# A decode kernel's down projection as row-streaming matmuls, with the last residual formed in four rows

## The chip, the cores and the metric

The kernel runs on one core of one Trainium2 chip. The metric is device time in microseconds of one execution. The engines are TensorE (PE; its weight loads are PEld), VectorE (DVE), ScalarE (ACT), GpSimd (POOL) and SyncE (SP). SyncE issues all the large loads. PSUM is the memory that TensorE writes its results to; a partition is one of the 128 rows of the on-chip memories. The granted clock is the share of TensorE's full clock that the profile shows. In the profile's lines, SPq and ACTq are the queues of SyncE and ScalarE, here with a DMA that they issue, and "issue" is time in which an engine waited for nothing that the profile shows. kt_sb is a large buffer that holds several small tiles of the changed kernel.

## The reference, cut to what matters

One token passes through adaptive layer norm, attention over a cache of 65,536 keys with 4 key/value heads, and a gated feed-forward block. Only the end of it matters here:

```python
x = x + ga * A_ref(h, ...)                       # attention, all before the change
h = layernorm(x) * (1 + cb) + sb
x = x + gb * ((gelu(h @ w_gate) * (h @ w_up)) @ w_down)     # w_down: 3584 x 1024, bf16
```

The result is one vector of 1024 bf16 numbers, 2 KB.

## The kernel before

The gate and up projections already work by rows: the activation column sits in a weight block of 32 columns (one used, 31 zero), the weight matrix's row is streamed against it 512 columns at a time, and four such matmuls go to the four groups of 32 PSUM partitions (four column tiles). The down projection does not: each 128x128 block of `w_down` is loaded as the stationary operand and meets a single column.

```python
def col_matvec(bank, jobs, rhs, ready, nblk):            # the down projection before
    ...
    for (jb, view, k0, nk) in jobs:
        PE.wait(jb.tok)                                  # this load has landed
        for kk in range(nk):
            for j in range(nblk):                        # 8 blocks of 128 columns
                ins = pe.matmul(bank[:, j:j+1], view[:, kk, j*P:(j+1)*P],
                                rhs[:, k0+kk:k0+kk+1], ...)
...
v = col_matvec(acc_dn, j_d, u_col, (v_uc,), KD)          # acc_dn: 128 x 8 in PSUM
t_dn  = acc_dn * gb_nat                                  # VectorE, 128 x 8
y_col = t_dn + x1_nat                                    # VectorE, 128 x 8
pe.transpose(b6[0:KD, 384:384+P], y_col, identf)         # to 8 rows of 128
y_row = copy(b6[0:KD, 384:384+P])                        # VectorE, to bf16
sp.dma_start(out[0, 0].rearrange("(j p) -> j p", p=P), y_row[:, :])   # partitions 0..7
```

(The last lines are simplified: the instructions are written as formulas, and the waits are left out; every step waits for the one above.) `w_down` has 28 rows of 128x1024. It comes in three loads of 8 rows (2 MB) and three small ones of 2, 1 and 1 rows. All are issued long before they land.

## Time and profile before

| | before |
|---|---|
| time, median of 3 runs | 440.44 us (440.28 to 440.68) |
| bytes read | 185.6 MB, 423 GB/s on average |
| last weight packet lands | 435.71 us |
| last down row starts on TensorE | 436.04 us |
| first VectorE instruction after it | 436.46 us |
| store issued | 437.60 us |
| end of span | 438.84 us |

Rows three to seven come from the records of DMA packets and instructions in the trace, counted from the start of the span. The store's own time, issue to end, is 438.84 - 437.60 = 1.24 us.

From the page of the kernel before: the first line gives the DMA engines' busy share in tenths of 40 slices, the last one the shares of the chain of work that ended last.

```profile
DMA  8999999999999999999999999999999999999995
...
DMA 60%; PE 35%; DVE 2%; issue 1%; SPq 1%; ACT 1%; POOL 0%
```

The DMA engines are busy at 90% or more in 38 slices of 40. Nothing that shortens TensorE's work in the middle can move the end much; only the last microseconds can.

The chain of waits of the kernel before, its end, in order of time (start us, length us, what):

```profile
404.33 29.13 DMA slots<-in_B_w_down_dram
...
433.51 2.51 PE b L372 x88
...
436.04 0.39 PE b L372 x8
...
436.46 0.18 DVE t_dn L844
...
436.66 0.18 DVE y_col L846
...
436.88 0.39 PE b L848
...
437.29 0.28 DVE y_row L850
```

The timeline of the kernel before (start us, length us, engine, line, operation, operands, shapes, count, and in brackets the idle time before and what ended it), its down groups and the store:

```profile
423.86 1.85 PE L372 MATMUL b<-u_col,slots 128*128 128x1 bf16 x64 [0.49 <-DVE u_col L841]
...
428.64 1.86 PE L372 MATMUL b<-u_col,slots 128*128 128x1 bf16 x64 [2.93 <-DMA slots<-in_B_w_down_dram]
...
433.51 2.91 PE L372 MATMUL b<-u_col,slots 128*128 128x1 bf16 x96 [3.01 <-DMA slots<-in_B_w_down_dram]
...
437.60 0.37 SPq L852 DMA_DIRECT2D out_dram<-y_row  x1
```

TensorE needs 1.85 us for 8 rows that take 4.8 us to arrive, and idles 3 us before the second and the third group. In the last group it has just caught up with the small loads. The windows view (us, busy us of each engine with its count of instructions, granted clock, DMA share, GB/s) shows the loads ending only while the last group runs:

```profile
435.50:436.00 0.50, 0.50 (x20) 0.43 (x17) 0.00 (x0) 0.00 (x0) 0.00 (x0) 0.50 0.17 49
436.00:437.00 1.00, 0.51 (x10) 0.38 (x9) 0.34 (x2) 0.00 (x0) 0.00 (x0) 0.50 0.00 0
```

So the end is a sum of steps after one event: the last weight lands; 0.34 us later the last row starts; 0.41 us later VectorE starts; 1.14 us of VectorE and transpose; 1.24 us of store.

### The profile page before, as it was taken

The page shows a single profiled execution, that of the slowest core. Times are in us where ns is not written, and L with a number is a line of the kernel's source. Part 1 is how long each engine was busy: PE and PEld are TensorE (multiplying, and loading weights), DVE is VectorE, ACT ScalarE, POOL GpSimd, SP SyncE. Part 2 cuts the span into 40 slices and gives each one's busy share as a digit, 9 for nine tenths or more (in the row PEclk, how much of TensorE's full clock was granted, in tenths as well). Part 3 has the DMA queues.
Part 4 walks back from the last instruction along what each step waited for, and adds up shares of the span by engine and source line. Part 5 has one row for each costly group of instructions (what it writes and reads, how often), then busy time and mean ns, then how long its engine had stood idle before and what let it go on. Part 6 is the DMA issues. An engine that isn't in the chain of part 4 may idle for free.

```text
span 438.8 us, 15336 instructions
## 1 busy us (share of the span) xinstructions
PE 351.7 (80%) x7107; PEld 318.4 (73%) x7107; DVE 176.2 (40%) x300; ACT 146.4 (33%) x553; POOL 11.7 (3%) x25
## 2 busy tenths in 40 slices
PE   0547449998989889898799989999989999557554
PEld 0214139998989879798799989899988999434234
DVE  4102013545444644455444466345563365142100
ACT  1000001343435634344613553444654434600000
POOL 8100000000000000000000000000000000000000
PEclk9955555959777986869955899556995597659855
DMA  8999999999999999999999999999999999999995
GB/s 332 427 435 428 430 429 432 432 433 425 430 445 420 453 414 455 408 445 438 410 448 415 445 419 442 427 435 432 430 437 424 439 423 433 432 427 431 424 425 237
DMA packets 11957, 185.89 MB, mean 424 GB/s; under 512 B 1568, under 2 KB 1568, under 8 KB 1952
## 3 DMA queue, kind: packets, MB, share of 16 engines
q1 hardware_dynamic: 11632, 185.61, 98.8%
q8 instruction: 13, 0.21, 0.2%
q10 hardware_dynamic: 304, 0.01, 0.0%
q14 instruction: 8, 0.07, 0.0%
HBM read 185.60 MB, written 0.00 MB: 423 GB/s over the span
## 4 chain that ended last, share of the span: by engine, by line
DMA 60%; PE 35%; DVE 2%; issue 1%; SPq 1%; ACT 1%; POOL 0%
DMA slots<-in_A_v_cache_dram 39%; PE kt_ps L561 18%; DMA slots<-in_A_k_cache_dram 10%; DMA slots<-in_B_w_down_dram 7%; PE b L625 7%; PE sc_ps L581 6%; DMA slots<-in_w_mod_dram 4%; PE kt_ps L392 2%; PE b L605 1%; SPq L234 1%; PE b L372 1%; ACT p_sb L691 1%; PE b L595 1%; DVE kt_sb L751 0%; PE sc_ps L453 0%
## 5 line engine op out<-in xcount | busy, mean ns | idle before, releaser
L561 PE MATMUL kt_ps<-ident,slots 128*128 128x128 bf16 x2048 | 179.5, 258 | 11.0 <-DMA slots<-in_A_k_cache_dram 10.3
L561 PEld LDWEIGHTS kt_ps<-ident,slots 128*128 128x128 bf16 x2048 | 154.9, 118 | 12.7 <-issue 9.8
L660 DVE COPY kt_sb<-kt_ps 128x2048 bf16<-128x2048 bf16 x96 | 117.6, 1225 | 108.6 <-PE kt_ps L561 108.5
L660 ACT ACTIVATE kt_sb<-kt_ps 128x2048 bf16<-128x2048 bf16 x32 | 60.1, 1877 | 183.3 <-PE kt_ps L561 183.3
L625 PE MATMUL b<-p_sb,slots 128*128 128x8 bf16 x2176 | 75.8, 168 | 20.6 <-DMA slots<-in_A_v_cache_dram 11.2
L625 PEld LDWEIGHTS b<-p_sb,slots 128*128 128x128 bf16 x2176 | 69.8, 100 | 23.3 <-DMA slots<-in_A_v_cache_dram 12.3
L691 ACT ACTIVATE p_sb<-sc_ps,mneg 128x64 bf16<-128x64 f32 x256 | 83.5, 560 | 3.9 <-DVE mneg L686 3.9
L691 ACT ACTIVATION_READ_ACCUMULATOR p_sb<-sc_ps,mneg 128x1 f32 x256 | 77.1, 365 | 0.0
L581 PE MATMUL sc_ps<-q_buf,kt_sb 128*128 128x8 bf16 x2112 | 69.9, 167 | 0.5 <-issue 0.5
L581 PEld LDWEIGHTS sc_ps<-q_buf,kt_sb 128*128 128x128 bf16 x2112 | 67.9, 100 | 0.6 <-issue 0.6
L392 PE MATMUL kt_ps<-slots,h_pad 128*32 128x512 bf16 x176 | 17.1, 510 | 14.3 <-DMA slots<-in_A_wq_dram 6.3
L684 DVE TENSOR_REDUCE mg<-b 8x1 f32<-8x128 f32 x32 | 8.9, 279 | 37.1 <-PE b L595 37.1
L679 DVE TENSOR_REDUCE m_col<-sc_ps 128x8 f32<-128x512 f32 x32 | 21.8, 681 | 4.7 <-PE sc_ps L581 4.7
L392 PEld LDWEIGHTS kt_ps<-slots,h_pad 128*32 128x32 bf16 x176 | 5.0, 112 | 24.1 <-DMA slots<-in_A_wq_dram 8.3
L392 PE MATMUL kt_ps<-slots,s_pad 128*32 128x512 bf16 x96 | 12.5, 553 | 9.3 <-DMA slots<-in_w_mod_dram 9.3
L392 PEld LDWEIGHTS kt_ps<-slots,s_pad 128*32 128x32 bf16 x96 | 3.6, 119 | 17.3 <-DMA slots<-in_w_mod_dram 12.6
L605 PE MATMUL b<-negi,mg 8*128 8x8 f32 x66 | 15.8, 309 | 0.0
L605 PEld LDWEIGHTS b<-negi,mg 8*128 8x128 f32 x66 | 12.7, 239 | 2.2
L453 PEld LDWEIGHTS sc_ps<-identf,kt_sb 128*128 128x128 f32 (+1 forms) x48 | 7.6, 204 | 8.2 <-DVE kt_sb L774 4.3
L453 PE MATMUL sc_ps<-identf,kt_sb 128*128 128x128 f32 (+1 forms) x48 | 9.1, 352 | 4.5 <-DVE kt_sb L774 2.4
L686 DVE COPY mneg<-b 128x8 f32<-128x8 f32 x32 | 5.3, 167 | 18.1 <-PE b L605 18.1
L372 PE MATMUL b<-u_col,slots 128*128 128x1 bf16 x224 | 6.6, 165 | 6.5 <-DMA slots<-in_B_w_down_dram 5.9
(97 smaller groups left out, 84.9 us busy)
## 6 DMA issues: line engine op xcount, KB each, us to landing
slots<-in_A_k_cache_dram SPq DMA_DIRECT2D x16, 4096.0 KB, 20.3
slots<-in_A_v_cache_dram SPq DMA_DIRECT2D x32, 2048.0 KB, 26.5
slots<-in_w_mod_dram SPq DMA_DIRECT2D x8, 1536.0 KB, 17.5
slots<-in_A_wq_dram SPq DMA_DIRECT2D x4, 2048.0 KB, 35.2
slots<-in_A_wo_dram SPq DMA_DIRECT2D x4, 2048.0 KB, 32.5
slots<-in_B_w_gate_dram SPq DMA_DIRECT2D x4, 1792.0 KB, 21.9
slots<-in_B_w_up_dram SPq DMA_DIRECT2D x4, 1792.0 KB, 23.6
slots<-in_B_w_down_dram SPq DMA_DIRECT2D x3, 2048.0 KB, 29.1
```

Of the source, the lines that this page charges most:

```text
L372: ins = pe.matmul(bank[:, j:j + 1], view[:, kk, j * P:(j + 1) * P], rhs[:, k0 + kk:k0 + kk + 1], start=first, stop=True, skip_group_check= ...
L392: ins = pe.matmul(out, pad[:, k, :], jb.view[:, kk, c0:c0 + ROW], start=k <= last_k[0], stop=k >= last_k[1], skip_group_check=True,)
L453: ins = pe.transpose(dst[:, i * w:i * w + n], src[:, a], identf[0:src.shape[0], 0:n])
L561: ins = pe.transpose(kt_ps[:, half * 2048 + t * P:half * 2048 + (t + 1) * P], j_k[i - i % KU].view[:, i % KU * CH + b * TB + t, :], ident[ ...
L581: ins = pe.matmul(sc_ps[:, base + n * REP:base + (n + 1) * REP], kt_sb[:, j % 2, n, :], q_buf[:, j % SITES, :], start=True, stop=True,)
L605: ins = pe.matmul(b6[:, 256:256 + REP], mg8[:, j % 2:j % 2 + 1].to_broadcast([REP, P]), negi[:, :], start=True, stop=True,)
L625: ins = pe.matmul(b7[:, s * REP:(s + 1) * REP], j_v[j].view[:, n, :], p_sb[:, s, n, :], start=(n == 0), stop=(n == CH - 1),)
L660: ev[i % SITES][b].done(act.activation(dst, src, ACT.Copy) if E_ is AC else dve.tensor_copy(dst, src))
L679: m1[s].done(dve.tensor_reduce(m_col[:, j % 2, :].unsqueeze(2), scv, AX.X, ALU.max))
L684: m2[s].done(dve.tensor_reduce(mg8[:, j % 2:j % 2 + 1], b6[0:REP, 32:32 + P], AX.X, ALU.max))
L686: v_mc[j] = DVE.done(dve.tensor_copy(mneg[:, j, :], b6[:, 256:256 + REP]))
L691: ins = act.activation(p_sb[:, s, :, h], scv[:, h, :], ACT.Exp, bias=mneg[:, j, h:h + 1], scale=scale, accum_out=z_all[:, j, h:h + 1],)
```

## The change

The intent: the down projection works by rows too, like the other projections. Each row of `w_down` streams in four matmuls of 256 columns, one to each group of 32 PSUM partitions. The result then lies in four rows, on partitions 0, 32, 64 and 96, so it needs no transpose. The residual and its gate are turned into the same four rows ahead of time. The diff, cut to its core:

```diff
+    for n, a in enumerate((gb_nat, x1_nat)):             # ahead of time: gate and residual,
+        for h in range(2):                               # spread to columns 0, 32, 64, 96
+            v_pq = DVE.done(dve.tensor_copy(
+                pad_q[:, (2*n+h)*P:(2*n+h+1)*P:QD], a[:, h:KD:2]))
 ...
-        for dst, a, b in zip(parts(u_col), parts(g2), parts_ps()):
+        for dst, a, b in zip(parts(o_pad[:, 0:FD, 0]), parts(g2), parts_ps()):
 ...
-        v = col_matvec(acc_dn, j_d, u_col, (v_uc,), KD)
+        for n in range(4):                               # before the first down row
+            ins = pe.transpose(kt_fp[...], pad_q[:, n*P:(n+1)*P], identf[:, :])
+        v_q4 = DVE.done(dve.tensor_copy(ktf(0)[:, 4*HALF:6*HALF], kt_fp[...]))   # gb_q, x1_q
+        def place_d(k):
+            for g in range(NQ):
+                yield acc_dn[QD*g:QD*(g+1), :], g*HALF
+        v = row_matvec(place_d, j_d, o_pad, (v_uc,), (0, FD-1), width=HALF)   # HALF = 256
-        v = DVE.done(dve.tensor_tensor(t_dn[:, :], acc_dn, gb_nat[:, :], ALU.mult))
-        v = DVE.done(dve.tensor_tensor(y_col[:, :], t_dn[:, :], x1_nat[:, :], ALU.add))
-        v = PE.done(pe.transpose(b6[0:KD, 384:384+P], y_col[:, :], identf[:, :]))
-        v = DVE.done(dve.tensor_copy(y_row[:, :], b6[0:KD, 384:384+P]))
-        sp.dma_start(out[0, 0].rearrange("(j p) -> j p", p=P), y_row[:, :])
+        v = DVE.done(dve.tensor_tensor(t_q, acc_dn, gb_q, ALU.mult))      # 128 x 256
+        v = DVE.done(dve.tensor_tensor(y_q, t_q, x1_q, ALU.add))          # to bf16
+        sp.dma_start(out[0, 0].rearrange("(g n) -> g n", g=NQ), y_q[0:P:QD, :])
 ... (waits cut; several small tiles move into a large buffer that is free by then)
```

`y_q[0:P:QD, :]` reads partitions 0, 32, 64, 96.

## The prediction

> **What bounds the kernel now.** The loads. The page gives 185.9 MB at 424 GB/s mean; the DMA engines stand at 9 tenths in 38 of 40 slices, and the chain of waits is 60% DMA and 35% TensorE, the latter mostly in the attention loop, which stays. Only the last microseconds can change: the down projection and what follows.
>
> There, TensorE waits for weights. By the timeline the three large down loads are used from 423.8, 428.6 and 433.5 us. A 64-matmul group takes 1.85 us of a 4.8 us interval, so TensorE idles about 3 us before each. After 433.5 the chain of waits lists 88 matmuls (2.51 us), then the last 8 (436.04 to 436.43). These start after a small gap: the windows view shows DMA still moving 49 GB/s in 435.5–436.0 and nothing after. So even the end of TensorE's work hangs on the last weight's landing (about 435.7), not on matmul throughput. Then, serial and exposed: multiply 0.17, add 0.17, transpose 0.37, cast 0.28, with gaps 436.46 to 437.57 = 1.11 us; then the store, to 438.8.
>
> **What the change does.**
> - Removes 224 one-column matmuls (28 rows x 8, about 27 ns apart: 0.21 us a row, clock 0.5 in the windows view).
> - Adds 112 matmuls of 256 columns, four column tiles at a time. At this clock 14 of the up projection's 512-column matmuls take 1.89 us, a group of four each 0.427 us. Estimate for 256 columns: half, 0.213 us a row: a tie. The Trainium skill, "TensorE: Matmul & The Clock Gate", Part 3, says column tiles run concurrently; this trace agrees. I expect the clock to stay at 0.5: TensorE still idles 60% of each interval.
> - The last row: four 256-column matmuls, about 0.39 us (first cold 512-column matmul 0.61 less 0.21), against 0.39 for eight small ones. A tie too.
> - After it: transpose and cast go; multiply and add grow from 8 to 256 columns. The 128x256 f32 multiply at the attention's end took 0.41 us; the Trainium skill, "VectorE: DVE Perf Modes", errata section, gives (N+151)/0.96 ns, an estimate of 0.42. So 0.42+0.42+gaps = 0.88 us instead of 1.11: about -0.23 us.
> - Off the path: zeroing and four small copies (near 403.7–405, VectorE idle until 406.9), four transposes (about 0.65 us) ahead of the first down group, a 0.69 us copy. The first group ends near 426.4 instead of 425.7; the next load comes at 428.6. Free.
> - Loads, order and slot releases are unchanged, so the stream ends when it did. The store has four 512 B rows instead of eight of 256 B: no difference expected (1.2 us from issue to end).
>
> **Prediction.** 440.44 - 0.23 = 440.2 us, range 439.5 to 440.9 (before's runs spread 0.4 us). Faster by over 2%: 0.005; within 2%: 0.99; slower by over 2%: 0.005.
>
> **What would show the steps.** Down groups of 32 matmuls taking about 1.9 us, TensorE still waiting about 2.9 us for each load; two VectorE instructions of about 0.42 us after the last matmul, 0.9 us from its end to the store's issue; clock 0.5 from 413 us; last weight packet near 435.7.
>
> **What would make it wrong.** If a 256-column row took well over 0.23 us (weight loads not hidden), the last 12 rows would lag behind the landing: 0.02 us for each 2 ns of a row. At clock 1 the last row would shorten by about 0.1 us. A shift in when the 16 DMA engines finish (last packets spread over 4 us) could move the end by several tenths either way.

## The result, and the profile after

The changed kernel takes 440.79 us (median of 6 runs, 440.65 to 440.99); the kernel before 440.44 us in 6 runs (440.28 to 440.68). The ratio is 1.0009 with a 95% interval of 0.9996 to 1.0021. A ratio here is the mean time of one kernel's fast runs over that of the other's fast runs of the same rounds, so it is not quite the ratio of the medians quoted. By the 2% rule the two are the same, and the interval includes 1. But the six runs of each barely overlap (before goes up to 440.68, after starts at 440.65), and the medians moved up, not down: +0.35 us where -0.23 was forecast. The outputs are right.

The chain of waits of the changed kernel, its end:

```profile
403.28 30.59 DMA slots<-in_B_w_down_dram
...
433.91 2.95 PE b L373 x25
...
436.89 0.43 DVE kt_sb L841
...
437.35 0.42 DVE kt_sb L843
```

The transpose and the cast are gone, and the two VectorE instructions have grown as forecast. The timeline of the changed kernel, its down groups and the store:

```profile
424.46 1.42 PE L373 MATMUL b<-slots,o_pad 128*32 128x256 bf16 x32
...
429.03 1.90 PE L373 MATMUL b<-slots,o_pad 128*32 128x256 bf16 x32 [3.14 <-DMA slots<-in_B_w_down_dram]
...
433.91 2.92 PE L373 MATMUL b<-slots,o_pad 128*32 128x256 bf16 x48 [2.99 <-DMA slots<-in_B_w_down_dram]
...
437.80 0.65 SPq L845 DMA_DIRECT2D out_dram<-kt_sb  x1
```

TensorE still idles some 3 us before the second and the third group, so the four transposes in front of the first group cost nothing. The last line is the surprise: issuing the store took 0.65 us where it took 0.37. SyncE then waited for it, by its own waits view, first of the kernel before and then of the changed one:

```profile
SPq L853 <- DMA out_dram<-y_row: 0.8, 1, 0.8
```

```profile
SPq L846 <- DMA out_dram<-kt_sb: 1.0, 1, 1.0
```

The granted clock of the changed kernel (third number from the end of a line), windows view:

```profile
424.00:426.00 2.00, 1.89 (x35) 1.06 (x33) 0.78 (x3) 0.00 (x0) 0.00 (x0) 0.69 1.00 422
426.00:428.00 2.00, 0.00 (x0) 0.00 (x0) 0.00 (x0) 0.00 (x0) 0.00 (x0) 1.00 1.02 430
428.00:430.00 2.00, 0.97 (x20) 0.75 (x24) 0.00 (x0) 0.00 (x0) 0.00 (x0) 0.67 1.00 422
430.00:433.00 3.00, 0.92 (x20) 0.33 (x12) 0.00 (x0) 0.00 (x0) 0.00 (x0) 0.50 1.00 412
```

It rose for a while, by the clock's own records from 425.3 to 428.7 us: rows 5 to 8 of the first group started 0.11 us apart instead of 0.21, so that group took only 1.42 us. It was back at 0.5 before the second group began, and stayed there for the group that counts.

All kernels can be laid side by side by the steps after the last weight's landing. The times (us) are differences of records in the trace: end of the last weight packet, start of the last row's first matmul, start of the first VectorE instruction after it, issue of the store, end of the span. The table includes the experiments of the next section.

| kernel | landing | landing to row | row to VectorE | VectorE to issue | issue to end | time, median |
|---|---|---|---|---|---|---|
| before | 435.71 | 0.34 | 0.41 | 1.14 | 1.24 | 440.44 |
| before, again (e10) | 435.92 | 0.34 | 0.41 | 1.14 | 1.24 | 440.55 |
| after | 436.09 | 0.35 | 0.46 | 0.91 | 1.70 | 440.79 |
| after, again (e11) | 435.92 | 0.37 | 0.46 | 0.91 | 1.69 | 440.88 |
| e1: after, 256 B pieces | 435.98 | 0.34 | 0.46 | 0.91 | 1.75 | 440.77 |
| e2: before, rows 16 partitions apart | 435.85 | 0.39 | 0.41 | 1.26 | 1.75 | 441.29 |
| e3: before, 4 adjacent rows | 435.85 | 0.34 | 0.41 | 1.49 | 1.23 | 440.83 |
| e4: after, ScalarE's queue | 436.15 | 0.38 | 0.46 | 0.91 | 1.71 | 440.95 |
| e5: after, adjacent (wrong) | 435.81 | 0.42 | 0.46 | 0.91 | 1.24 | 440.43 |
| e6: after, 4 one-row stores | 436.17 | 0.34 | 0.46 | 0.91 | 1.69 | 440.84 |
| e7: before, residual in PSUM | 435.72 | 0.38 | 0.41 | 0.90 | 1.24 | 440.13 |
| e8: e7 and idle matmuls | 435.74 | 0.37 | 0.41 | 0.90 | 1.24 | 440.11 |
| e9: before, rows 2 partitions apart | 436.06 | 0.35 | 0.41 | 1.15 | 1.83 | 441.03 |

From before to after: last row +0.05, VectorE to issue -0.23, store +0.46, together +0.28 us. The times differ by 0.35. The remaining 0.07 is within the scatter of the landing (more on that under e10 and e11). All of the store's extra time lies before its first packet: by the records that came 0.79 us after the issue began in the kernel before and 1.25 in the changed one, and from there to the end it took 0.44 and 0.45.

### The profile page after: what moved, and what is told of

It is laid out like the page before. It is cut to its first block, busy times and chain, and to the rows that moved or that the text cites. A ratio compares the mean times of both kernels' runs of the same rounds, so it can differ in the third digit from the quotient of the medians.

```text
span 439.5 us, 15124 instructions
## 1 busy us (share of the span) xinstructions
PE 344.2 (78%) x6998; PEld 309.0 (70%) x6998; DVE 177.2 (40%) x305; ACT 146.5 (33%) x553; POOL 11.7 (3%) x25
## 4 chain that ended last, share of the span: by engine, by line
DMA 60%; PE 34%; DVE 2%; issue 2%; SPq 1%; ACT 1%; POOL 0%
DMA slots<-in_A_v_cache_dram 40%; PE kt_ps L542 17%; DMA slots<-in_A_k_cache_dram 10%; DMA slots<-in_B_w_down_dram 7%; PE b L606 7%; PE sc_ps L562 6%; DMA slots<-in_w_mod_dram 4%; PE kt_ps L373 2%; PE b L586 1%; SPq L231 1%; PE b L373 1%; ACT p_sb L672 1%; PE b L576 1%; DVE kt_sb L732 0%; PE sc_ps L434 0%
## 5 line engine op out<-in xcount | busy, mean ns | idle before, releaser
L542 PE MATMUL kt_ps<-ident,slots 128*128 128x128 bf16 x2048 | 173.3, 253 | 14.0 <-DMA slots<-in_A_k_cache_dram 13.3
L542 PEld LDWEIGHTS kt_ps<-ident,slots 128*128 128x128 bf16 x2048 | 149.2, 115 | 15.8 <-issue 10.1
L606 PE MATMUL b<-p_sb,slots 128*128 128x8 bf16 x2176 | 74.9, 167 | 23.8 <-DMA slots<-in_A_v_cache_dram 11.3
L606 PEld LDWEIGHTS b<-p_sb,slots 128*128 128x128 bf16 x2176 | 68.8, 99 | 26.6 <-issue 13.3
L586 PE MATMUL b<-negi,mg 8*128 8x8 f32 x66 | 14.9, 296 | 0.0
L757 ACT ACTIVATE kt_sb<-kt_ps 96x512 f32<-96x512 f32 (+1 forms) x3 | 1.8, 594 | 30.8 <-PE kt_ps L373 30.8
```

The source lines that it names most:

```text
L542: ins = pe.transpose(kt_ps[:, half * 2048 + t * P:half * 2048 + (t + 1) * P], j_k[i - i % KU].view[:, i % KU * CH + b * TB + t, :], ident[ ...
L586: ins = pe.matmul(b6[:, 256:256 + REP], mg8[:, j % 2:j % 2 + 1].to_broadcast([REP, P]), negi[:, :], start=True, stop=True,)
L606: ins = pe.matmul(b7[:, s * REP:(s + 1) * REP], j_v[j].view[:, n, :], p_sb[:, s, n, :], start=(n == 0), stop=(n == CH - 1),)
```

## The experiments

The theory after the first comparison: the store got dearer because its rows no longer lie on adjacent partitions. Its rivals: there are fewer rows (four instead of eight); the pieces are larger (512 B instead of 256 B); the state of SyncE's queue; chance in one profile; and, outside the store, that the wide rows on TensorE or the later landing cost the time.

A difference of 0.4 us is 0.1% of the time, and the intervals of the ratios below are some 0.13 to 0.17% on each side. So the ratios of single experiments settle next to nothing here (of all of them only e2's interval excludes 1). The steps in the trace after the last row's start repeat to about 0.02 us where nothing was changed in them.

### e1: the same four partitions, in pieces of 256 B

```diff
-    y_q = ...[:, 0:HALF]                        # 256 adjacent numbers
+    y_q = ...rearrange("p (h n) -> p h n", h=2)[:, :, 0:P]      # two runs of 128, with a gap
-        sp.dma_start(out[0, 0].rearrange("(g n) -> g n", g=NQ), y_q[0:P:QD, :])
+        sp.dma_start(out[0, 0].rearrange("(g h n) -> g h n", g=NQ, h=2), y_q[0:P:QD, :, :])
```

> The changed kernel with one edit: the store still reads partitions 0, 32, 64, 96, but each row leaves as two pieces of 256 B. The profile of the changed kernel has 1.70 us from the store's issue to the end of the span (issue 0.65), that of before 1.24 (issue 0.37). Theory 'four rows' (the cost comes with the count of four rows): still about 1.7. Theory 'spread partitions' (it comes with the step of 32 partitions): still about 1.7. Theory 'piece size' (it comes with 512 B pieces): about 1.24. Theory 'chance' (one profile was unlucky): about 1.24, and different from one run to the next.

The timeline of this kernel, the store:

```profile
437.69 0.69 SPq L848 DMA_DIRECT2D out_dram<-kt_sb  x1
```

The store stayed dear: issue 0.69 us, 1.75 us to the end; 440.77 us against 440.40 of before in the same rounds, ratio 1.0007 (0.9990 to 1.0023). The DMA records show eight packets of 256 B. Piece size alone is out, and so is chance.

### e2: the kernel before, with its rows 16 partitions apart

```diff
-    y_col = sb("y_col", [P, KD])
+    y_wide = ktf(0)[:, 0:P]                     # zeroed beforehand
+    y_col = y_wide[:, 0:P:P // KD]              # columns 0, 16, .., 112
-    y_row = sb("y_row", [KD, P], dt.bfloat16)
+    y_row = ktf(0)[:, P:2*P].bitcast(dt.bfloat16)[:, 0:P]   # in the buffer that y_q uses
-        pe.transpose(b6[0:KD, 384:384+P], y_col[:, :], identf[:, :])
+        pe.transpose(b6[:, 384:384+P], y_wide, identf[:, :])
 ... (the cast's 128 rows and the waits cut)
-        sp.dma_start(..., y_row[:, :])
+        sp.dma_start(..., y_row[0:P:P // KD, :])
```

> The kernel before with one edit: its eight rows of 256 B lie on partitions 0, 16, .., 112 instead of 0 to 7 (the transpose takes a zero-padded 128-column operand, so it may cost some 0.05 to 0.1 us more). 'Four rows': issue to end stays 1.24 us, issue 0.37. 'Spread partitions': about 1.7, issue 0.65. 'Piece size': 1.24. 'Chance': 1.24.

The timeline of this kernel, its transpose and its store:

```profile
core 0 of [0], span 439.7 us
...
437.07 0.48 PE L851 MATMUL b<-identf,kt_sb 128*128 128x128 f32 x1 [0.47 <-DVE kt_sb L849]
...
437.91 0.71 SPq L855 DMA_DIRECT2D out_dram<-kt_sb  x1
```

With the kernel before's eight rows of 256 B, its arithmetic and its down matmuls, the step between partitions took the issue from 0.37 to 0.71 us, and issue to end from 1.24 to 1.75. The rows also moved to another buffer here; e3 and e5 read adjacent partitions of that same buffer and are cheap, so the buffer is out as a cause. The wider transpose added 0.1 us, the upper end of what was expected. The time was 441.29 us against 440.40, ratio 1.0020 (1.0003 to 1.0036).

### e3: the kernel before, with four rows of 512 B on adjacent partitions

```diff
-    y_row = sb("y_row", [KD, P], dt.bfloat16)
+    y_row = ktf(0)[0:NQ, 0:P].bitcast(dt.bfloat16)          # 4 x 256, in the buffer that y_q uses
-        v = PE.done(pe.transpose(b6[0:KD, 384:384+P], y_col[:, :], identf[:, :]))
+        for h in range(2):
+            ins = pe.transpose(kt_fp[0:NQ, (8+h)*P:(9+h)*P], y_col[:, h:KD:2], identf[:, :])
+        v = PE.done(ins)
-        sp.dma_start(out[0, 0].rearrange("(j p) -> j p", p=P), y_row[:, :])
+        sp.dma_start(out[0, 0].rearrange("(j p) -> j p", j=NQ), y_row)
```

> The kernel before with one edit: the last transpose is made in two halves so that four rows of 512 B lie on adjacent partitions 0 to 3. 'Four rows': issue to end about 1.7 us, issue 0.65. 'Spread partitions': 1.24, issue 0.37. 'Piece size': about 1.7. 'Chance': 1.24. The cast of 256 columns should take about 0.42 us instead of 0.28 and the second transpose add about 0.1.

The timeline of this kernel, its cast and its store:

```profile
core 0 of [0], span 439.3 us
...
437.65 0.41 DVE L853 CAST kt_sb<-kt_ps 4x256 bf16<-4x256 f32 x1 [0.68 <-PE kt_ps L849]
438.09 0.35 SPq L855 DMA_DIRECT2D out_dram<-kt_sb  x1
```

Four rows of 512 B are as cheap as eight of 256 B when they are adjacent: 0.35 us to issue, 1.23 to the end. "Four rows" and "piece size" are out. The median was higher than before's (440.83 against 440.40; ratio 1.0009, 0.9992 to 1.0025), and the trace shows where: a second transpose and a longer cast made VectorE-to-issue 1.49 us. The cast grew as expected, but the two transposes took 0.59 us where one took 0.37, so the second cost twice the expected 0.1.

### e4: the changed kernel, store issued by ScalarE

```diff
-        SP.wait(v); sp.dma_start(...); sp.wait_ge(out_sem, 16)
+        AC.wait(v); act.dma_start(...); act.wait_ge(out_sem, 16)
```

> The changed kernel with one edit: the store is issued from ScalarE's queue, which has been idle since the up projection's eviction, instead of from SyncE's queue, which carried all the loads. If the longer store comes from the state of SyncE's queue after the loads, issue to end falls to about 1.2 us. If it comes from the shape of the store, it stays about 1.7. Also a further look at when the last weight lands in the changed kernel: 436.1 us in its one profile against 435.7 before; if that is chance, it scatters by some tenths over these four runs without regard to the kernel.

The timeline of this kernel, the store:

```profile
437.90 0.62 ACTq L845 DMA_DIRECT2D out_dram<-kt_sb  x1
```

The idle queue was no better: issue 0.62, 1.71 us to the end, 440.95 against 440.40 us. The state of SyncE's queue is out. This agrees with the Trainium skill, "DMA: Bandwidth & Descriptors", section "Issuing engines are not separate DMA queues", by which the DMAs of all issuing engines run on the same DMA engines; which of them carried this store, the trace does not show.

### e5: the changed kernel, store from adjacent partitions (wrong)

```diff
-        sp.dma_start(out[0, 0].rearrange("(g n) -> g n", g=NQ), y_q[0:P:QD, :])
+        sp.dma_start(out[0, 0].rearrange("(g n) -> g n", g=NQ), y_q[0:NQ, :])
```

Three of its four output rows hold no result. It shows what the rest of the change is worth.

> The changed kernel with one edit, wrong on purpose: the store reads partitions 0 to 3 instead of 0, 32, 64, 96, so three of the four rows hold no result; it measures what the change would be worth without the step between its partitions. 'Spread partitions': issue to end falls from 1.70 to 1.24 us (issue 0.35), the time by about 0.46 us, from 440.79 to about 440.3, a little below before (440.42). 'The wide rows on TensorE cost it' (rival: the loss sits in the matmuls or in the weights' landing, not in the store): the time stays near 440.8.

The timeline of this kernel, the last row and what follows:

```profile
core 0 of [0], span 438.8 us
...
436.23 0.41 PE L373 MATMUL b<-slots,o_pad 128*32 128x256 bf16 x4 [0.17 <-DMA slots<-in_B_w_down_dram]
436.69 0.42 DVE L841 TENSOR_TENSOR kt_sb<-b,kt_sb 128x256 f32<-128x256 f32 x1 [11.73 <-PE b L373]
437.15 0.42 DVE L843 TENSOR_TENSOR kt_sb<-kt_sb 128x256 bf16<-128x256 f32 x1
437.60 0.35 SPq L845 DMA_DIRECT2D out_dram<-kt_sb  x1
```

With the change's whole arithmetic kept, issue fell to 0.35 and issue to end to 1.24 us, about the figures of before (0.37 and 1.24). The time was 440.43 us, beside 440.48 of before in the same rounds (ratio 1.0000, 0.9987 to 1.0014) and 440.79 of the changed kernel. The rival that put the loss into the wide rows falls; what the trace leaves to them is the 0.05 us of the last row. The store's step fell by the expected 0.46 us, the median by only 0.36. In this profile the last row started 0.07 us later after the landing than in after's (0.42 against 0.35); the rest is within the spread of the five runs (440.19 to 440.66). The run also shows TensorE waiting for the last weight ("[0.17 <-DMA ...]"), so the wide rows keep up with the loads.

### e6: the changed kernel, four stores of one row

```diff
+        for E_, q, gs in ((SP, sp, (0, 1)), (AC, act, (2, 3))):
+            E_.wait(v)
+            for g in gs:
+                q.dma_start(rows[g:g+1, :], y_q[QD*g:QD*g+1, :]).then_inc(out_sem, 16)
+        sp.wait_ge(out_sem, 64)
```

> The changed kernel with one edit: four stores of one row each, two from SyncE's queue and two from ScalarE's, so that none has a step between partitions. If the step alone makes a store dear, each issue takes about 0.35 us, two in a row 0.75, and issue to end is 1.24 + about 0.38 = 1.6 us, 0.1 less than the changed kernel's 1.70. If every store from partitions 32, 64, 96 is dear whatever its step, issues take about 0.65 and issue to end is over 2.2 us.

The timeline of this kernel, its stores by queue:

```profile
437.88 0.62 SPq L848 DMA_DIRECT2D out_dram<-kt_sb  x2
437.88 0.56 ACTq L848 DMA_DIRECT2D out_dram<-kt_sb  x2
```

Each single-row issue took 0.25 to 0.32 us, even from partitions 32, 64 and 96, so those partitions are not dear in themselves; the step within one store is. But two issues in a row ate the gain: 1.69 us from issue to end, not the expected 1.6, and 440.84 us (ratio 1.0007, 0.9992 to 1.0022). By the records the end came 0.50 us after the last packet, where it took 0.36 to 0.37 in the kernels before and after. The semaphore updates in the trace show where that arose: the completions of the four stores arrived 1.11, 1.30, 1.48 and 1.66 us after the first issue, 0.18 to 0.19 us apart, although the packets of the first two had ended within 0.03 us of each other. What spaces them is open.

### e7: the kernel before, with the residual put into PSUM ahead of time

The store of before is the good one, so the search for something faster than both goes from there. The transpose is a matmul, and a matmul can accumulate: the residual is turned into rows ahead of the first down row (at 423.2 us), and the last matmul adds the scaled projection to it.

Simplified in the same way:

```diff
+        pe.matmul(b6[0:KD, 384:384+P], x1_nat[:, :], identf[:, :], start=True, stop=False, ...)
         v = col_matvec(acc_dn, j_d, u_col, (v_uc,), KD)
         t_dn = acc_dn * gb_nat                               # now rounded to bf16
-        y_col = t_dn + x1_nat
-        pe.transpose(b6[0:KD, 384:384+P], y_col[:, :], identf[:, :])
+        pe.matmul(b6[0:KD, 384:384+P], t_dn[:, :], ident[:, :], start=False, stop=True, ...)
```

> The kernel before with one edit that keeps its store: the residual is put into the transpose's PSUM rows while TensorE waits for weights (an f32 matmul against the identity), and the scaled projection, rounded to bf16, is added there by one bf16 matmul against the identity. The add (0.17 us and its gap 0.03) goes and the f32 transpose of 0.37 us becomes a cold bf16 matmul of 128 columns (estimate 0.29, from 0.39 for a cold 256-column one less 0.107). From the last matmul's end to the store's issue: about 0.85 us instead of 1.14, so about 440.1 us, 0.28 below before.

The timeline of this kernel, after the last down group:

```profile
core 0 of [0], span 438.7 us
...
436.52 0.17 DVE L845 TENSOR_TENSOR t_dn<-b,gb_nat 128x8 bf16<-128x8 f32 x1 [12.83 <-PE b L371]
...
436.74 0.27 PE L848 MATMUL b<-ident,t_dn 128*8 128x128 bf16 x1 [0.26 <-DVE t_dn L845]
437.11 0.28 DVE L851 CAST y_row<-b 8x128 bf16<-8x128 f32 x1 [0.43 <-PE b L848]
437.42 0.37 SPq L853 DMA_DIRECT2D out_dram<-y_row  x1
```

VectorE to issue fell to 0.90 us (0.85 was expected), as short as in the changed kernel, with the cheap store kept. The result is correct. The time was 440.13 us (440.01 to 440.42) beside 440.48 (440.25 to 440.57), ratio 0.9995 (0.9981 to 1.0009). The interval includes 1, so the times do not show it faster; the trace does show the step that is shorter, by 0.24 us.

### e8: e7 with idle matmuls to raise the clock

```diff
                 release(jb, tok)
+                for _ in range(fill_in[n] if n < len(fill_in) else 0):      # 6, then 7
+                    pe.matmul(kt_fp[:, 0:ROW], ident[:, :], slots[8][:, 0:ROW], ...)
```

> As the run before, and 6 and 7 idle matmuls of 512 columns into a free bank after the first two down groups, to bring TensorE's clock to 1 before the last group. If the clock rises, the last 8 matmuls take about 0.3 us instead of 0.39 and the bf16 matmul about 0.2 instead of 0.29: another 0.15 to 0.2 us, about 439.9. If the clock stays at 0.5, the idle matmuls (7 x 0.427 = 3.0 us in a wait of 3.0) can push the last group back by some tenths, and the run is slower than the one before it.

The windows view of this kernel, around the down groups:

```profile
426.00:428.00 2.00, 2.00 (x5) 0.58 (x4) 0.00 (x0) 0.00 (x0) 0.00 (x0) 0.50 1.03 434
428.00:430.00 2.00, 1.66 (x51) 1.35 (x51) 0.00 (x0) 0.00 (x0) 0.00 (x0) 0.50 0.98 406
430.00:433.00 3.00, 2.76 (x26) 1.25 (x24) 0.00 (x0) 0.00 (x0) 0.00 (x0) 0.50 0.97 401
433.00:436.50 3.50, 3.36 (x98) 2.71 (x96) 0.00 (x0) 0.00 (x0) 0.00 (x0) 0.50 0.35 136
```

The clock stayed at 0.50 although TensorE's records fill 9.78 of these 10.5 us. The steps are those of e7 and the time, 440.11 us, too (ratio 0.9995, 0.9981 to 1.0009). The idle matmuls neither helped nor pushed the last group back. What would raise the clock there is open.

### e9: the kernel before, with its rows 2 partitions apart

As e2, with a step of 2: `y_col = y_wide[:, 0:2*KD:2]`, and the store reads `y_row[0:2*KD:2, :]`.

> The kernel before with its eight rows of 256 B on partitions 0, 2, .., 14. The store of rows 16 partitions apart took 1.75 us from issue to end (issue 0.71), adjacent ones 1.24 (0.37). If any step over 1 is dear: about 1.75 again. If what is dear is that the rows lie in different groups of 32 partitions: 1.24. From the last down matmul to the store's issue about 1.15 us, as before.

The timeline of this kernel, the store:

```profile
core 0 of [0], span 439.8 us
...
437.97 0.79 SPq L855 DMA_DIRECT2D out_dram<-kt_sb  x1
```

All the rows lie within one group of 32 partitions, and still the issue took 0.79 us and issue to end 1.83. The time was 441.03 us against 440.45 (ratio 1.0011, 0.9994 to 1.0028). So it is a step of more than one partition, even 2, and not the spread over partition groups.

### e10 and e11: both kernels again, unchanged

> The kernel before, unchanged, for a second profile: store 1.24 us from issue to end, last weight at 435.7 to 435.9 if the five profiles of its family so far (435.71 to 435.85) are typical; up to 436.2 if the landing is chance alone.

> The changed kernel, unchanged, for a second profile: store 1.70 us from issue to end, 0.91 us from the last matmul to the issue, 0.46 for the last row. The five profiles of its family so far have the last weight at 435.81 to 436.17; near 436.1 would mean that these builds' loads run some 0.2 us late from the start, near 435.8 that it is chance.

Every step after the last row's start repeated to within 0.01 us (table above). The last weight landed at 435.92 us in both profiles, where the first pair had 435.71 and 436.09. So the two pairs do not show that the change makes the landing later. The medians were 440.55 and 440.88 us, beside 440.45 of before in the same rounds.

The landing still leaves a small question. Five of the six profiles of the changed kernel's family lie at 435.92 or later; of the seven others only two do. In the first pair the lag was there early: 2% of the bytes of the load queue had landed at 11.70 us in before and at 11.88 us in after, before any changed instruction had run. In the second pair it was 11.74 and 11.79.

Sorted by the store instead of the family, the 13 profiles split more clearly. In the seven kernels whose store has a step or is in four pieces (after, e1, e2, e4, e6, e9, e11), the first small load, of the vector c, landed at 6.96 to 7.26 us and the last weight at 435.85 to 436.17, 436.03 on average. In the six with one store from adjacent partitions (before, e3, e5, e7, e8, e10) these were 4.87 to 5.23 and 435.71 to 435.92, 435.79 on average. So the builds differ from the start, in step with the form of a store that comes last, and some tenths of the landing may go with it. No run tells why, and the steps after the last row's start are not touched by it.

## Why the prediction was right or wrong

- **Range and class: right, the range by its width.** 440.79 us lies in 439.5 to 440.9, and the change is within 2%. But the range is 1.4 us wide, and a change of +0.35 fits into it as well as the -0.23 that was argued for.
- **Sign: wrong.** It forecast -0.23 us; the measured medians give +0.35 and, repeated, +0.33 (440.88 - 440.55), and the steps in the trace sum to +0.28.
- **The step that failed:** "The store has four 512 B rows instead of eight of 256 B: no difference expected (1.2 us from issue to end)." Count and size of the rows indeed made no difference (e3: 1.23 us). But the rows are also 32 partitions apart, and that term was missing: 1.70 instead of 1.24 us, +0.46 us on the critical path. It turned up when the step was put into before (e2, e9) and went when it was taken out of after (e5).
- **A smaller term mis-sized:** the last row, called a tie at 0.39 us. From its start to VectorE's start it took 0.46 us in all six profiles of wide rows and 0.41 in all seven others: +0.05.
- **VectorE to issue: right.** It fell from 1.14 to 0.91 us, with two instructions of 0.42 us. The estimate came from a 128x256 multiply elsewhere in the trace (0.41 us) and from the formula of the Trainium skill, "VectorE: DVE Perf Modes", errata section. For 256 columns that gives an estimate of 0.424 us, and the records say 424 ns for both.
- **TensorE in the middle: right.** A group of 32 wide matmuls took 1.90 us at clock 0.5, and four column tiles overlap, as the Trainium skill, "TensorE: Matmul & The Clock Gate", Part 3, says: the four matmuls of the last row start within 0.01 us. TensorE waited some 3 us for the second and the third load.
- **Clock at 0.5 from 413 us: wrong, without effect.** It stood at 1 until 415.0 us, rose again in the first down group (425.3 to 428.7) and was back before the second.
- **Preparation off the path: right.** Zeroing, copies, transposes and the 0.69 us copy fell into waits.
- **Landing: right within its scatter.** "Near 435.7": 436.09 and 435.92, against 435.71 and 435.92 of before. That the two builds load alike from the start is not quite so (e10 and e11).

## What to carry to other kernels

When the end of a kernel hangs on the last load, list the steps after the landing one by one; a change pays only through that list, and a matmul form that does the same row in the same time pays nothing. Cost the store with its access pattern, not its bytes: here a step between partitions took 0.46 to 0.59 us more than adjacent partitions for the same 2 KB, twice what dropping a transpose and a cast had won. A layout that saves a step of computing (rows where the column tiles left them) can be dear to store; where it is, accumulating the residual into the transpose's PSUM saved as much in the trace (e7: 0.24 us, with a total time not clear of noise) and left the rows adjacent.

## What the Trainium skill lacked or had wrong

- "DMA: Bandwidth & Descriptors" gives no cost for a step between the partitions of a DMA. Here a 2 KB store with a step of 2, 16 or 32 partitions took 0.62 to 0.79 us to issue and 1.69 to 1.83 us from issue to end; with adjacent partitions 0.35 to 0.37 and 1.23 to 1.24. Its section "Latency and other measured facts" has about 600 ns to the first byte, without saying from when: here the first packet came 0.79 us after the issue began in the kernel before and 1.25 us with the step of 32. What takes the extra time, no run here shows.
- The same page names 512 B as the least transfer for full rate. That is a statement on rate and is not refuted; in the time of a store this small no difference was seen: eight rows of 256 B took 1.24 us, four of 512 B 1.23.
- "TensorE: Matmul & The Clock Gate", Part 1, has the clock rise after some 3.4 us of sustained activity, but does not say whether matmuls of one column count. In e8 TensorE's records filled 9.78 of 10.5 us with one-column matmuls and 13 idle wide ones in turn, and the clock stayed at 0.50. In the changed kernel it rose to 1 during the first down group, after 3.35 us of transposes and wide rows without a pause (421.91 to 425.26). So busy time in the records alone did not decide it here; what did, no run settles.
